# Weaving the two halves of the MLP weights in a fused attention and mixer kernel

## The chip, the cores and the metric

The kernel runs on one core of a Trainium2 chip. The metric is the device time of one execution in microseconds (us). Each TensorE product is two instructions in the trace: a weight load (LDWEIGHTS, row "PEld"), which puts the stationary operand into the array, and a MATMUL (row "PE"), which streams the moving operand past it. The other engines are VectorE (DVE), ScalarE (ACT), GpSimd (POOL) and SyncE (SP), whose queue issues the transfers.

## The reference, cut to what matters

Three layers follow each other. Attention with tanh-capped scores gives x for 2 batches of 448 tokens with 768 channels. The second layer is the one that the change touches:

```python
X = np.fft.fft(np.fft.fft(x, axis=1), axis=2)
u = x + np.real(X)
un = (u - mean(u)) / np.sqrt(var(u) + 1e-06)
x = u + np.maximum(un @ w_ch1, 0.0) @ w_ch2      # w_ch1 768x3072, w_ch2 3072x768
```

The third layer is a gated spatial mixer with weights w_in, w_sg and w_out. The weights w_ch1, w_ch2, w_in and w_out come as 64-bit floats; everything is computed in 32 bits.

## The kernel before, in words

**One product is three.** [...] `product` (L172) issues, for each block of 128 input channels, upper times upper, upper times lower and lower times upper, each with its own weight load. In the MLP the weights are the stationary operand, 128 by 128 words, and the tokens are the moving operand, 448 columns.

**Weights.** `w_ch1` is cut into 24 blocks of 128 columns (`columns`, L844), `w_ch2` into 24 blocks of 128 rows (`rows`, L852). The number f0 of a block runs from 0 to 23 in both; the trace calls both `w_<f0>` (with `raw` and `cvt` behind it for the stages of the conversion). `weight` (L799) makes one block: a transfer of the 64-bit words, then seven steps (`size` to `lower`) which shift and mask the words into 32 bits and write the upper half (`upper`, L828) and the lower half (`lower`, L831) into the tile `w`. That tile holds 768 words of upper halves and behind them 768 words of lower halves in each partition:

```python
w = wpool[tag].tile([P, 2, NP * P], F32R, tag=tag, bufs=W_BUFS[tag], name=tile_name)   # L808
```

`upper` runs on ACT, except for w1_0 to w1_3, w2_0 and w2_1, where it is a DVE copy. `lower` runs on DVE.

**Order.** The MLP is done in six groups of four blocks. In a group, `hidden` (tile h, four blocks of `w_ch1`, L857) and then `mixed` (tile c, four blocks of `w_ch2`, L869) run for batch 0 and batch 1. Each block takes part in 36 products in each of its two roles, so 72 for one f0 and 1728 in all. Group 0 is interleaved by hand with the Fourier transforms and the layer norm of batch 1 (the long list at the end of the `bounded` branch); groups 1 to 5 are ordered by the framework. A weight tile has four buffers per pool (two in "wc"), so a conversion starts when an older block has been read for the last time and its transfer has landed.

**Addresses.** `FILL` (L64) puts small pads between pools. With them, the stationary tile and the moving tile of every product of 448 columns and 128 rows in the MLP start 64 bytes apart, counted modulo 256. In the tile of `v` they start 32 bytes apart. [...]

The functions of the program that the change touches, and what calls them:

Of the kernel before, what the change touches and what calls it, by code (L numbers as in the profile page):

```python
# [13 lines left out]
F32R = mybir.dt.float32r  # L14
# [7 lines left out]
P = 128  # L22
B, H, S, D = 2, 12, 448, 64
C = H * D
NP = H // 2
# [35 lines left out]
W_BUFS = {"wa": 4, "wb": 4, "wc": 2}  # L61


FILL = {"const": 288, "wb": 96, "normed0": 224, "hidden0": 96, "wc": 96}  # L64
EDGE, GATE_ROW, TABLE_ROW = 160, 192, 3776


# [21 lines left out]
def f32(ap):  # L89
    return ap.bitcast(F32)  # L90
# [9 lines left out]
def common_part(ctx, tc, q, k, cap):  # L100
# [5 lines left out]
    edge = ctx.enter_context(tc.tile_pool(name="edge", bufs=1, side="right"))  # L106
    fill = const.tile([P, FILL["const"] // 4], F32, tag="fill", bufs=1, name="fill_const")
    ident = const.tile([P, P], F32, name="ident")
# [23 lines left out]
def attention_mixers_kernel(ctx, tc, bounded, common, q, k, v, cap, w_ch1, w_ch2, w_in, g_ln, w_sg, b_sg, w_out,  # L132
                            t1, t2, out):
    nc = tc.nc
    w_ch1, w_ch2, w_in, w_out = (w.bitcast(U32) for w in (w_ch1, w_ch2, w_in, w_out))
# [4 lines left out]
    def fill(pool, name):  # L140
        t = pool.tile([P, FILL[name] // 4], F32, tag="fill", bufs=1, name=f"fill_{name}")
        nc.gpsimd.memset(t[:, 0:1], 0.0)
# [651 lines left out]
    def fetch(tile_name, src, lead, width):  # L794
        raw = wraw.tile([P, 2 * NP * P], U32, tag="raw", bufs=2, name=f"{tile_name}raw")
        sp.dma_start(raw[:, :2 * lead * width].rearrange("p (k f) -> p k f", k=lead), src)
        return raw

    def weight(tile_name, src, lead, width, tag, lo_engine=None, pin=False, raw=None, hi_copy=None, pieces=None):  # L799


        n = lead * width
        if raw is None:
            raw = fetch(tile_name, src, lead, width)
        words = raw[:, :2 * n].rearrange("p (n w) -> p n w", w=2)
        low, high = words[:, :, 0], words[:, :, 1]
        c = wraw.tile([P, NP * P], U32, tag="cvt", bufs=2, name=f"{tile_name}cvt")[:, :n]
        w = wpool[tag].tile([P, 2, NP * P], F32R, tag=tag, bufs=W_BUFS[tag], name=tile_name)  # L808

        def size():  # L810
            first_op = act.activation(f32(c), f32(high), AF.Abs)
            if pin:
                tc.keep_in_program_order(first_op)

        def clamp():
            vec.tensor_scalar(f32(c), f32(c), LEAST, MOST, op0=ALU.max, op1=ALU.min)

        def shift():
            vec.tensor_scalar(c, c, 5, 2, op0=ALU.logical_shift_left, op1=ALU.logical_shift_right)

        def top():
            vec.scalar_tensor_tensor(c, high, 0xC0000000, c, op0=ALU.bitwise_and, op1=ALU.bitwise_or)

        def bottom():
            vec.scalar_tensor_tensor(c, low, 29, c, op0=ALU.logical_shift_right, op1=ALU.bitwise_or)

        def upper():
            (hi_copy or act.copy)(w[:, 0, :n], f32(c))  # L828

        def lower():  # L830
            (lo_engine or vec).tensor_tensor(w[:, 1, :n], f32(c), f32(w[:, 0, :n]), op=ALU.subtract)  # L831

        steps = size, clamp, shift, top, bottom, upper, lower
        if pieces is None:
            for step in steps:
                step()
        else:
            pieces.extend(steps)
        return w

    def column_block(src, f0):
        return src[:, 2 * f0 * P:2 * (f0 + 1) * P].rearrange("(k p) f -> p k f", p=P)

    def columns(src, f0, name, tag="wa", **how):  # L844

        w = weight(f"{name}{f0}", column_block(src, f0), NP, P, tag, **how)
        return w.rearrange("p a (k f) -> p a k f", k=NP)

    def row_block(src, f0):
        return src[f0 * P:(f0 + 1) * P, :].unsqueeze(1)  # L850

    def rows(src, f0, name, tag="wb", **how):  # L852

        return weight(f"{name}{f0}", row_block(src, f0), 1, C, tag, **how)


    def hidden(b, g, un, w1, hs, chunks=range(GF)):  # L857
# [170 lines left out]
    def opened(*names):  # L1028
        pools = [ctx.enter_context(tc.tile_pool(name=name, bufs=1)) for name in names]
        for pool, name in zip(pools, names):  # L1030
            if name in FILL:
                fill(pool, name)
        return pools if len(pools) > 1 else pools[0]

    wraw = opened("wraw")
    wpool = {"wa": opened("wa")}
# [11 lines left out]
    with ExitStack() as fctx:  # L1048
# [8 lines left out]
        with ExitStack() as actx:  # L1057
# [8 lines left out]
            if bounded:  # L1066
                f, n0 = fourier(0, fp, t2sb, POOL_FOLDS[0]), layer_norm(0, fp)
                f1, n1 = fourier(1, fp, t2sb), layer_norm(1, fp)
                raws, pieces = {}, {}
                do = functools.partial  # L1070

                def get(*key):
                    name, i = key
                    src = column_block(w_ch1, i) if name == "w1_" else row_block(w_ch2, i)
                    raws[key] = fetch(f"{name}{i}", src, *((NP, P) if name == "w1_" else (1, C)))

                def convert(*key):
                    name, i = key
                    how = dict(raw=raws[key], pieces=pieces.setdefault(key, []))
                    if name == "w1_":  # L1080
                        w1.append(columns(w_ch1, i, name, hi_copy=vec.tensor_copy, **how))
                    else:
                        w2.append(rows(w_ch2, i, name, hi_copy=None if i > 1 else vec.tensor_copy, **how))
# [48 lines left out]
            else:  # L1132
# [5 lines left out]
                for n in range(n_pairs + 2):  # L1138

                    if n + 2 < n_pairs:  # L1140
                        raws[n + 2] = load(*pairs[n + 2])
                    for step, group in enumerate(GROUPS):
                        if n < n_pairs:
                            es[n, step] = score(*pairs[n], step, *ready[n])
                        if 0 < n <= n_pairs:
                            if step == 0:
                                pTs[n - 1] = ap.tile([CP, NT, ROWS * P], F32, tag="pT", bufs=2, name=f"pT{n - 1}")
                            for i, r in enumerate(group):
                                flip(*pairs[n - 1], r, i, es[n - 1, step], pTs[n - 1])
                        if step == 1 and n > 1:  # L1150
                            values(*pairs[n - 2], raws[n - 2][2], pTs[n - 2])
                            if pairs[n - 2] == (0, NP - 1):
                                side = norm(0, fp, t2sb)
                        if step == 1 and n + 1 < n_pairs:
                            ready[n + 1] = prepare(*pairs[n + 1], n + 1, raws[n + 1])
                        for f in range(GF):
                            if (n, step) == W1_AT[f]:
                                w1.append(columns(w_ch1, f, "w1_", lo_engine=pool, pin=f < 2))
                        run(side, SIDE_STEPS[step])
# [119 lines left out]
        else:  # L1279
# [10 lines left out]
            run(main, 2)  # L1290
            run(side, 2)
            w2.extend(rows(w_ch2, f, "w2_", pin=True) for f in range(GF))
            w1_next = [columns(w_ch1, GF + f, "w1_", "wc", pin=True) for f in range(2)]
            for n_side, n_main in PLAN:
                run(main, n_main)
# [14 lines left out]
    for g in range(1, NG):  # L1310
# [24 lines left out]
        if g == 2:  # L1335
# [3 lines left out]
            sp.dma_start(sg_raw[:, :, :S], rows_sg)  # L1339
            sp.dma_start(sg_raw[:, :, S:], rows_sg[:, :, NB * P:])  # L1340
        w2 = [rows(w_ch2, g * GF + f, "w2_") for f in range(GF)]
        for b in range(B):
            if g == NG - 1:
# [9 lines left out]
    for j in range(2):  # L1353
        for k in range(2):
            block = w_in[k * HC:(k + 1) * HC, 2 * DH + j * 512:2 * DH + (j + 1) * 512]
            w = weight(f"wv{j}{k}", block.rearrange("(k p) f -> p k f", p=P), 3, 256, "wb")
            wv.append(w.rearrange("p a (k f) -> p a k f", k=3))
# [45 lines left out]
```

## Time and profile before

| | |
|---|---|
| median of 2 runs | 615.39 us (615.38 to 615.41) |
| the profiled execution's own time | 616.05 us |
| its span in the trace | 614.3 us |
| granted TensorE clock, mean | 0.998 |
| PE busy | 603.2 us, 98% |
| PEld busy | 517.6 us, 84% |
| DVE busy | 481.1 us, 78% |
| ACT busy | 271.0 us, 44% |
| POOL busy | 111.5 us, 18% |

A MATMUL's duration in the trace is longer than the time until the next one starts, since they are pipelined. The distance from start to start is therefore read from a run of equal instructions: the time from the first start to the last end, less the duration of one, divided by the count less one. In the chain of waits such a run stands as one piece with its count, which is already that distance times the count.

### The profile page before, as it was taken

To read this page: it belongs to the slowest core of one execution; us is meant where nothing else is said; L and a number is where in the kernel's file an instruction comes from. 1 tells how busy PE (TensorE), PEld (TensorE's weight loads), DVE (VectorE), ACT (ScalarE), POOL (GpSimd) and SP (SyncE) were. 2 spreads that over 40 slices of the span, in tenths; PEclk is the share of its full clock that TensorE was granted. 3 is DMA by queue.
4 is the path that set the end of the run, shared out by engine and by line. 5 is a ranking of instruction groups with operands and counts; after the bars stand their busy time and mean duration, and the time that the engine had idled before them with its cause. 6 is when DMAs were issued, how large, how long until landed. Compare 5 with 4: busy or idle time off the path is not lost.

```text
span 614.3 us, 8700 instructions
## 1 busy us (share of the span) xinstructions
PE 603.2 (98%) x3324; PEld 517.6 (84%) x3324; DVE 481.1 (78%) x764; ACT 271.0 (44%) x374; POOL 111.5 (18%) x156
## 2 busy tenths in 40 slices
PE   7999999999999999999999999999999999999995
PEld 5455566469999999999999999999999999989985
DVE  2698988889876898998938973885579899898461
ACT  5999876932132344334304422350245254543231
POOL 2889895552000000000000000000000010100000
PEclk9999999999999999999999999999999999999999
DMA  6766732201100447444413440453044204100123
GB/s 161 178 172 168 204 91 53 100 0 53 53 1 16 155 155 205 159 157 156 154 52 103 130 179 0 126 177 110 1 161 147 104 24 140 44 1 2 35 71 80
DMA packets 70034, 62.61 MB, mean 102 GB/s; under 512 B 36256, under 2 KB 63840, under 8 KB 69984
## 3 DMA queue, kind: packets, MB, share of 16 engines
q1 hardware_dynamic: 69056, 61.74, 32.7%
q8 instruction: 28, 0.46, 0.3%
q10 hardware_dynamic: 928, 0.23, 0.2%
q14 instruction: 22, 0.18, 0.1%
HBM read 59.21 MB, written 2.75 MB: 101 GB/s over the span
## 4 chain that ended last, share of the span: by engine, by line
PE 89%; DVE 4%; ACT 2%; DMA 2%; issue 1%; POOL 1%; SPq 0%; DVEq 0%; ACTq 0%
PE c L178 28%; PE h L178 26%; PE v L178 5%; PE o L666 5%; PE out L178 5%; PE u L178 5%; PE s L640 4%; PE sg L178 2%; PE st L307 2%; PE st L266 1%; PE tr L605 1%; PE den L679 1%; PE den L677 1%; DMA w_0raw<-in_moe_w_ch 1%; DMA w_2raw<-in_moe_w_ch 1%
## 5 line engine op out<-in xcount | busy, mean ns | idle before, releaser
L178 PE MATMUL c<-h,w 128*128 128x448 f32 x864 | 175.5, 363 | 0.0
L178 PE MATMUL h<-un,w 128*128 128x448 f32 x864 | 174.9, 362 | 0.0
L178 PEld LDWEIGHTS c<-h,w 128*128 128x128 f32 x864 | 161.8, 187 | 11.5 <-DVE h L899 0.4
L178 PEld LDWEIGHTS h<-un,w 128*128 128x128 f32 x864 | 161.7, 187 | 11.5 <-ACT xT L671 0.7
L874 DVE TENSOR_TENSOR xT<-xT,c 128x448 f32<-128x448 f32 x60 | 36.9, 616 | 33.4 <-PE c L178 33.4
L1347 POOL CAST x<-x 128x384 fp32r<-128x384 f32 x2 | 2.8, 1423 | 315.5 <-PE u L178 315.5
L645 ACT ACTIVATE e<-s,tanh_scale 128x896 f32<-128x896 f32 (+1 forms) x48 | 40.9, 927 | 10.6 <-PE s L640 10.5
L666 PE MATMUL o<-e,v 128*64 128x448 f32 x192 | 42.0, 553 | 0.0
L658 POOL TENSOR_TENSOR t<-t,e 128x224 f32<-128x224 f32 x48 | 41.7, 897 | 0.1
L654 POOL TENSOR_TENSOR t<-e 128x224 f32<-128x224 f32 x48 | 40.6, 876 | 3.3 <-POOL mix L629 2.0
L649 ACT ACTIVATE e<-e,cap_pos 128x1792 f32<-128x1792 f32 (+1 forms) x24 | 37.9, 1632 | 0.0
L865 ACT ACTIVATE h<-h 128x448 fp32r<-128x448 f32 x40 | 21.7, 542 | 26.6 <-DVE h L866 16.5
L178 PE MATMUL out<-gated,wo 128*128 128x448 f32 x144 | 30.9, 367 | 0.0
L178 PEld LDWEIGHTS v<-wv,x 128*128 128x128 f32 x252 | 29.7, 188 | 0.1
L178 PE MATMUL v<-wv,x 128*128 128x256 f32 x252 | 29.7, 279 | 0.0
L178 PE MATMUL u<-x,wu 128*128 128x448 f32 x144 | 29.1, 362 | 0.0
L640 PEld LDWEIGHTS s<-qT,kT 64*128 64x128 f32 x216 | 19.4, 188 | 10.9 <-ACT e L649 4.2
L178 PEld LDWEIGHTS u<-x,wu 128*128 128x128 f32 x144 | 26.9, 187 | 1.8
L178 PEld LDWEIGHTS out<-gated,wo 128*128 128x128 f32 x144 | 26.3, 188 | 2.0 <-ACT gated L169 0.2
L640 PE MATMUL s<-qT,kT 64*128 64x448 f32 x216 | 27.3, 385 | 0.6 <-ACT qT L613 0.2
L866 DVE SCALAR_TENSOR_TENSOR h<-h,h 128x448 fp32r<-128x448 f32 x40 | 24.7, 618 | 1.8 <-ACT h L865 1.8
L666 PEld LDWEIGHTS o<-e,v 128*64 128x64 f32 x192 | 11.5, 136 | 16.4 <-issue 14.2
(405 smaller groups left out, 864.3 us busy)
## 6 DMA issues: line engine op xcount, KB each, us to landing
out<-res SPq DMA_DIRECT2D x12, 224.0 KB, 2.5
k<-in_k SPq DMA_DIRECT2D x22, 112.0 KB, 3.6
q<-in_q SPq DMA_DIRECT2D x22, 112.0 KB, 4.0
t<-dft_channels SPq DMA_DIRECT2D x8, 291.0 KB, 5.3
v<-in_v SPq DMA_DIRECT2D x24, 96.0 KB, 2.6
w_0raw<-in_moe_w_ch SPq DMA_DIRECT2D x2, 768.0 KB, 5.1
w_1raw<-in_moe_w_ch SPq DMA_DIRECT2D x2, 768.0 KB, 5.5
w_2raw<-in_moe_w_ch SPq DMA_DIRECT2D x2, 768.0 KB, 5.0
```

The lines of the kernel that those rows point to most:

```text
L178: pe.matmul(ps, lhs(i, a), rhs(i, b), start=start and m == 0, stop=stop and m == last)
L266: pe.matmul(ps[:HS, m * 256:m * 256 + NE], fold[:, i, m * HS:(m + 1) * HS], tab[:, i, :], start=i == 0, stop=i == 2)
L307: pe.matmul(sums[c][:, n * 256 + i:n * 256 + 2 * HS:2], src[:, i, sel], t2sb[:HS, n, i, :], start=True, stop=True)
L640: pe.matmul(ps[:, i, :S], t[lo:hi, x, at:at + P], qT[lo:hi, y, :], start=m == 0, stop=m == 2)
L645: act.activation(es[n][:, 2 * step:2 * step + nr], sums.pop((n, step))[:, :nr, :S], AF.Tanh, scale=tanh_scale)
L649: act.activation(part, part, AF.Exp, scale=cap_pos)
L654: pool.tensor_tensor(t[:, j, q], es[n][:, j, q], es[n][:, 2 + j, q], op=ALU.add)
L658: pool.tensor_tensor(ts[n][:, j, q], ts[n][:, j, q], es[n][:, 4 + j, q], op=ALU.add)
L666: pe.matmul(os[n][halfs[j], :S], vts[n % 3][:, j, i], es[n][:, 2 * i + j if i < 3 else 6], start=i == 0, stop=i == 3)
L865: act.activation(h[:, 0], ps[:, i, :S], AF.Relu)
L866: vec.scalar_tensor_tensor(h[:, 1], ps[:, i, :S], 0.0, f32(h[:, 0]), op0=ALU.max, op1=ALU.subtract)
L874: vec.tensor_tensor(u[:, c, :], u[:, c, :], ps[:, :S], op=ALU.add)
```

## The change

The tile of a weight block is 64 words (256 bytes) longer per partition. A new function, `halves_of`, gives the view of it in which the two halves are written and read. For `w_in` and `w_out` the view is as before. For a block f0 below 16 the view starts 4·f0 words (16·f0 bytes) into the tile and the halves alternate word by word: upper word 0, lower word 0, upper word 1, and so on. A weight load of 128 words thus takes every second word of 1024 bytes, where it took 512 bytes in a row. For the blocks 16 to 23 the halves stay one behind the other, and the view starts 16 times 0, 1, 2, 3, 4, 6, 8 and 12 bytes into the tile. No instruction is added or removed, and no loop changes.

```diff
+PLAIN = (0, 1, 2, 3, 4, 6, 8, 12)
...
+    def halves_of(w, place):
+
+        if place is None:
+            return w[:, :2 * NP * P].rearrange("p (a n) -> p a n", a=2)
+        at, woven = place
+        part = w[:, 4 * at:4 * at + 2 * NP * P]
+        return part.rearrange("p (n a) -> p a n", a=2) if woven else part.rearrange("p (a n) -> p a n", a=2)
+
...
-        w = wpool[tag].tile([P, 2, NP * P], F32R, tag=tag, bufs=W_BUFS[tag], name=tile_name)
+        w = halves_of(wpool[tag].tile([P, 2 * NP * P + 64], F32R, tag=tag, bufs=W_BUFS[tag], name=tile_name), place)
...
+    def place_of(src, f0):
+
+        if src is w_in or src is w_out:
+            return None
+        return (f0, True) if f0 < 16 else (PLAIN[f0 - 16], False)
+
...
-        w = weight(f"{name}{f0}", column_block(src, f0), NP, P, tag, **how)
+        w = weight(f"{name}{f0}", column_block(src, f0), NP, P, tag, place=place_of(src, f0), **how)
...
-        return weight(f"{name}{f0}", row_block(src, f0), 1, C, tag, **how)
+        return weight(f"{name}{f0}", row_block(src, f0), 1, C, tag, place=place_of(src, f0), **how)
```

## Rows read from the trace of the kernel before

**Rows 1.** The page, part 4: the chain's share by engine.
```profile
PE 89%; DVE 4%; ACT 2%; DMA 2%; issue 1%; POOL 1%; SPq 0%; DVEq 0%; ACTq 0%
```

**Rows 2.** Chain of waits, 200 to 500 us: start us, us, piece.
```profile
236.41 28.80 PE c L178 x144
265.21 28.81 PE h L178 x144
...
410.81 28.80 PE c L178 x144
439.61 28.81 PE h L178 x144
```

**Rows 3.** Busy time by stretch: PE, PEld, DVE, ACT, POOL, PEclk, DMA share, GB/s.
```profile
15.00:125.00 110.00, 108.90 (x673) 61.43 (x671) 94.08 (x141) 95.38 (x111) 87.22 (x114) 1.00 0.50 135
207.00:265.00 58.00, 58.00 (x291) 54.35 (x291) 52.03 (x77) 22.28 (x31) 0.00 (x0) 1.00 0.54 173
265.00:323.00 58.00, 58.00 (x292) 54.35 (x291) 44.79 (x65) 18.03 (x26) 0.00 (x0) 1.00 0.38 128
```

**Rows 4.** Groups by line: shapes, count | busy us, mean ns | idle before, releasers.
```profile
L187 PE MATMUL s<-mean_w 128*128 128x256 bf16 x12 | 1.5, 272 | 0.0
L266 PE MATMUL st<-t,fold 128*113 128x194 f32 x96 | 16.8, 329 | 0.2 <-DVE fold L254 0.2
L307 PE MATMUL st<-t2sb,back 113*128 113x113 f32 x48 | 5.9, 277 | 0.0
L178 PE MATMUL v<-wv,x 128*128 128x256 f32 x252 | 29.7, 279 | 0.0
```

**Rows 5.** Timeline of PE: start us, us, instructions of one kind in a row.
```profile
11.46 1.47 PE L187 MATMUL s<-mean_w 128*128 128x256 bf16 x12
...
151.44 2.14 PE L266 MATMUL st<-t,fold 128*113 128x194 f32 x12
...
160.27 2.84 PE L307 MATMUL st<-t2sb,back 113*128 113x113 f32 x24
...
553.13 12.77 PE L178 MATMUL v<-wv,x 128*128 128x256 f32 x108
```

**Rows 6.** Groups of DVE, 190 to 614 us.
```profile
L822 DVE SCALAR_TENSOR_TENSOR w_6cvt<-w_6raw,w_6cvt 128x768 uint32<-128x768 uint32 x2 | 1.9, 956 | 0.0
L831 DVE TENSOR_TENSOR w<-w_10cvt,w 128x768 fp32r<-128x768 f32 x2 | 1.9, 956 | 0.2 <-ACT w L828 0.2
```

**Rows 7.** Lines 828 and 811, instruction by instruction: ns min/median/max, starts.
```profile
L828 DVE CAST w<-w_0cvt x2: 659/664/669, 22.4 to 87.0; 128x768 fp32r<-128x768 f32 x2
L828 DVE CAST w<-w_1cvt x2: 829/864/900, 35.1 to 117.1; 128x768 fp32r<-128x768 f32 x2
L828 ACT CAST w<-w_4cvt x2: 828/830/833, 199.8 to 220.9; 128x768 fp32r<-128x768 f32 x2
...
L811 ACT ACTIVATE w_6cvt<-w_6raw x2: 902/906/910, 206.2 to 224.9; 128x768 f32<-128x768 f32 x2
```

**Rows 8.** Timeline around the fourth block of group 1, both roles.
```profile
217.01 0.95 DVE L831 TENSOR_TENSOR w<-w_7cvt,w 128x768 fp32r<-128x768 f32 x1
...
236.25 2.96 PE L178 MATMUL c<-h,w 128*128 128x448 f32 x14
236.43 0.96 DVE L831 TENSOR_TENSOR w<-w_7cvt,w 128x768 fp32r<-128x768 f32 x1 [0.90 <-ACT w L828]
```

**Rows 9.** Groups of DVE, 88 to 160 us: a write of every second word (L283).
```profile
L314 DVE TENSOR_TENSOR xT<-xT,st 128x225 f32<-128x225 f32 x8 | 3.1, 384 | 1.4 <-PE st L307 1.4
L283 DVE TENSOR_TENSOR pq<-st,late 113x194 f32<-113x194 f32 x8 | 2.4, 350 | 0.0
```

More of the change, by code (lines that the diff above doesn't have):

```diff
@@ L797, in fetch, with weight @@
         return raw
-    def weight(tile_name, src, lead, width, tag, lo_engine=None, pin=False, raw=None, hi_copy=None, pieces=None):
+    def halves_of(w, place):
[4 more added lines that the diff above has]
+        return part.rearrange("p (n a) -> p a n", a=2) if woven else part.rearrange("p (a n) -> p a n", a=2)
+    def weight(tile_name, src, lead, width, tag, lo_engine=None, pin=False, raw=None, hi_copy=None, pieces=None,
+               place=None):
         n = lead * width
```

## The prediction

> **What bounds the kernel now.** I read the chain of waits first: TensorE carries 89% of it [rows 1]. From 200 to 500 us the chain is nothing but runs of 144 products, each run 28.80 or 28.81 us [rows 2], so one product takes 200.0 ns from start to start, without a gap, whatever DVE and ACT do beside it. The busy table by stretch comes second: PE is full in those stretches, and DVE has 52.03 of 58 us in group 1 and less after it [rows 3]. So the change is worth what it does to those 200.0 ns, times the products that it touches, plus what it does to the conversions where they are nearly late.
>
> [...]
>
> [...]
>
> **The change, part by part.**
>
> 1. *Woven loads.* Blocks 0 to 15, 72 products each: 1152 of the 1728. No row shows a weight load that takes every second word, so I bound the price. [...] I take 0. The nearest rows for the load itself are DVE's reads of every second word: L822 takes 956 ns, L831 with whole rows of words takes 956 ns as well [rows 6]. [...]
>
> 2. *Plain blocks moved by 16 to 192 bytes.* Seven of the eight (block 16 stays at 0), 7 × 72 = 504 products. [...] I take 0: in the `st` products with 113 columns the operands start at changing distances, and 24 of them in a row hold 111.3 ns on average [rows 5]; they don't show a full-rate stream, so the bounds stay in the range.
>
> 3. *`upper` on DVE, six copies.* The four of w_0 and w_1 have medians of 664 and 864 ns [rows 7]. They might drop to the pace of a two-input operation, 956 ns [rows 6]: 2 × 292 + 2 × 92 = 0.8 us, and the two of w1_2 and w1_3 add at most 0.6 us. Not below 0, since the same words are moved. They lie in 15 to 125 us, where DVE has 94.08 of 110 us [rows 3] and the chain is mostly PE. Nearest row for the write: L283 writes every second word, 194 of them, in 350 ns; L314 writes 225 in a row in 384 ns [rows 9]. The 31 words fewer save 34 ns, 1.1 ns each, about the 1.2 ns per word of L822 (956 / 768, its fixed part included), so the step costs nothing. What may be lost is the copy's faster pace. I put 0.2 of the 1.4 us on the path.
>
> 4. *`upper` on ACT, 26 of its 42 copies become woven.* The nearest row for a step of two words on ACT is a read: 906 against 830 ns for a copy in a row [rows 7], so 0 to 76 ns each. Cost 0: ACT is idle for more than half of group 1 [rows 3]. The cover is thin at one place: block 7 as `w_ch1` is first read at 207.44 + 54 × 0.2 = 218.2 us and its lower half 0.4 us later, and it is ready at 217.96 [rows 2, 8]; as `w_ch2` it is the tenth product of the stage at 236.25, so 238.05, lower half 238.45, and ready at 237.39 [rows 8]. 0.7 and 1.1 us to spare against 0.08; if that cover went, PE would wait for the difference, once for each.
>
> 5. *`lower` on DVE.* It reads one woven half and writes the other; both steps are priced at 0 by rows 6 and 9. The transfers and SP's queue are not touched.
>
> Sum: 616.05 (the profiled execution's own time, 614.3 of span and 1.75 around it) + 0 + 0 + 0.2 = 616.25. The profiled execution is 0.66 us over the median of the runs, so in runs that is **615.6 us**.
>
> **The rivals.**
>
> *Full pace without loss (faster), 0.20.* [...] A part of this gain (only some of the 16 distances are good), 605 to 612 us, I give 0.12.
>
> *Twice the lines, twice the loss (slower), 0.17.* [...]
>
> *The load becomes the bound (slower), 0.06.* [...]
>
> *The plain blocks alone feel their new places, 0.05:* up to 5.5 us to either side, 610 to 621.
>
> *No price, my forecast, 0.40:* 615.6, by itself 612 to 619.
>
> **How the numbers follow.** 2% of the median, about what a measurement of this kernel can tell from no change, is 12.3 us: 603.1 and 627.7 us are the borders. The first rival ends astride the lower border; I count half of it, 0.10, as faster. The second ends just above the upper one; I count 0.10 of its 0.17 as slower, with all of the third: 0.16. Within 2%: 0.74. The range takes in the forecast, the partial gain, most of the first rival and the second, and leaves out the load as the bound: 602.5 to 628.5.
>
> **What would show it.** In the chain of waits after, the runs of 144 products of groups 1 to 3 (woven) against groups 4 and 5 (plain): my forecast has 28.8 us in all of them. [...] L828 on DVE should lie between today's time and 956 ns, on ACT between 830 and 906. I would be wrong if the start-to-start time in the woven groups moves by more than 3 ns, or if PE waits near 218 or 238 us.

## The result and the profile after

The changed kernel takes **622.89 us** (622.45 to 623.34, 2 runs) against 615.39: a ratio of **1.0122** with an interval of 1.0078 to 1.0165. That is slower, by less than the 2% of the prediction's border, and inside its range; the interval leaves no doubt that it moved. The profiled execution took 622.45 us, with 620.6 us of span at a mean granted clock of 0.998; the span is 6.3 us longer than before's. In the kernel after, the product stands in L179, `upper` in L838 and `lower` in L841.

The chain of waits of the kernel after, 200 to 510 us (start us, us, piece), answers to [rows 2]:

```profile
208.26 29.39 PE h L179 x144
237.65 29.36 PE c L179 x144
267.01 29.18 PE h L179 x144
296.20 29.27 PE c L179 x144
325.47 14.68 PE h L179 x72
340.15 1.54 PE sgT L1344 x16
341.68 14.67 PE h L179 x72
356.36 29.57 PE c L179 x144
385.92 29.31 PE h L179 x144
415.24 29.27 PE c L179 x144
444.51 29.32 PE h L179 x144
473.83 29.14 PE c L179 x144
```

Each piece still follows the one before it without a gap, but none has 28.80 us: a product comes every 202.4 ns (29.14 / 144) to 205.3 ns (29.57 / 144). The pieces of groups 1 to 3, which are woven, add up to 176.12 us, those of groups 4 and 5, plain, to 117.04 us. The same pieces added up to 172.86 and 115.22 us before, so the loss is 3.3 and 1.8 us. Group 0 loses 0.57 us: from the first `h` product to the first run above it is 76.25 us, and was 75.68. That is 5.7 of the 6.3 us. The stage ahead of the MLP is 0.1 us later, and the rest comes behind the last piece of the chain (`res` ends 5.99 us before the span does, 5.39 before).

Where the chain carries PE only, the engines beside it tell whether PE is starved. Timeline of PE in the kernel after, 208 to 240 us (start us, us, instructions in a row, idle time in brackets if any), answers to [rows 8]:

```profile
208.10 29.55 PE L179 MATMUL h<-un,w 128*128 128x448 f32 x144
237.49 2.82 PE L179 MATMUL c<-h,w 128*128 128x448 f32 x13
```

No bracket stands behind either row: PE waits neither near 218 nor near 238 us, the two places where the prediction had called the cover thin. Busy time by stretch of the kernel after, columns as in [rows 3]:

```profile
207.00:265.00 58.00, 58.00 (x286) 55.22 (x285) 52.00 (x75) 22.85 (x30) 0.00 (x0) 1.00 0.53 166
```

The granted clock is 1.00 as before [rows 3], and PE is still full, with 286 MATMULs in the 58 us where 291 stood. A full busy column says nothing about the pace.

Groups by line of the kernel after (columns as in [rows 4]), first MATMULs, then weight loads:

```profile
L179 PE MATMUL c<-h,w 128*128 128x448 f32 x864 | 178.2, 366 | 0.0
...
L179 PEld LDWEIGHTS c<-h,w 128*128 128x128 f32 x864 | 166.2, 193 | 9.9 <-PE c L179 0.2 <-issue 0.2
L179 PEld LDWEIGHTS h<-un,w 128*128 128x128 f32 x864 | 165.8, 192 | 10.4 <-ACT xT L672 0.7
...
L179 PEld LDWEIGHTS u<-x,wu 128*128 128x128 f32 x144 | 26.9, 187 | 1.8
```

The recorded load is 192 to 193 ns on the mean of woven and plain blocks, where the load of `u`, untouched, has 187. The plain blocks have no part in that: in groups 4 and 5 (390 to 500 us), where all are plain, the loads of `h` and `c` have 188, in the woven groups (210 to 380 us) 195.

Lines 838 and 841 of the kernel after, instruction by instruction (ns min/median/max, starts), answer to [rows 7] and [rows 6]; w_16 belongs to a plain block:

```profile
L838 DVE CAST w<-w_0cvt x2: 671/672/672, 22.4 to 87.1; 128x768 fp32r<-128x768 f32 x2
L838 DVE CAST w<-w_1cvt x2: 836/870/903, 35.2 to 117.1; 128x768 fp32r<-128x768 f32 x2
L838 ACT CAST w<-w_4cvt x2: 887/889/891, 200.3 to 221.9; 128x768 fp32r<-128x768 f32 x2
...
L838 ACT CAST w<-w_15cvt x2: 889/924/960, 298.2 to 332.5; 128x768 fp32r<-128x768 f32 x2
L838 ACT CAST w<-w_16cvt x2: 835/838/842, 345.4 to 384.1; 128x768 fp32r<-128x768 f32 x2
...
L841 DVE TENSOR_TENSOR w<-w_4cvt,w x2: 951/952/952, 201.6 to 223.1; 128x768 fp32r<-128x768 f32 x2
```

Over the 24 copies of the blocks 4 to 15, ACT has a mean of 901 ns, where it was 830: 70 ns more, and nine of the 26 woven copies on ACT lie above the 906 ns of the forecast. No product waits for one, so the conversions cost the kernel what was forecast, and nearly all of the loss is in the pace of the products.

### The profile page after: what moved, and what is told of

It is laid out like the page before. It is cut to its first block, busy times and chain, and to the rows that moved or that the text cites. A ratio compares the mean times of both kernels' runs of the same rounds, so it can differ in the third digit from the quotient of the medians.

```text
span 620.6 us, 8700 instructions
## 1 busy us (share of the span) xinstructions
PE 608.3 (98%) x3324; PEld 525.7 (85%) x3324; DVE 483.2 (78%) x764; ACT 272.6 (44%) x374; POOL 111.5 (18%) x156
## 4 chain that ended last, share of the span: by engine, by line
PE 90%; DVE 4%; DMA 2%; ACT 1%; issue 1%; POOL 1%; SPq 0%; DVEq 0%; ACTq 0%
PE c L179 28%; PE h L179 26%; PE o L667 5%; PE v L179 5%; PE out L179 5%; PE u L179 5%; PE s L641 5%; PE sg L179 2%; PE st L308 2%; PE st L267 1%; PE den L678 1%; PE den L680 1%; PE tr L606 1%; DMA w_0raw<-in_moe_w_ch 1%; DMA w_2raw<-in_moe_w_ch 1%
## 5 line engine op out<-in xcount | busy, mean ns | idle before, releaser
L179 PE MATMUL c<-h,w 128*128 128x448 f32 x864 | 178.2, 366 | 0.0
L179 PE MATMUL h<-un,w 128*128 128x448 f32 x864 | 177.9, 366 | 0.0
L179 PEld LDWEIGHTS h<-un,w 128*128 128x128 f32 x864 | 165.8, 192 | 10.4 <-ACT xT L672 0.7
L179 PEld LDWEIGHTS c<-h,w 128*128 128x128 f32 x864 | 166.2, 193 | 9.9 <-PE c L179 0.2
L179 PE MATMUL out<-gated,wo 128*128 128x448 f32 x144 | 30.9, 367 | 0.0
L179 PE MATMUL v<-wv,x 128*128 128x256 f32 x252 | 29.7, 279 | 0.0
L179 PEld LDWEIGHTS v<-wv,x 128*128 128x128 f32 x252 | 29.7, 188 | 0.1
L179 PE MATMUL u<-x,wu 128*128 128x448 f32 x144 | 29.1, 362 | 0.0
L179 PEld LDWEIGHTS u<-x,wu 128*128 128x128 f32 x144 | 26.9, 187 | 1.8
L179 PEld LDWEIGHTS out<-gated,wo 128*128 128x128 f32 x144 | 26.4, 188 | 2.0 <-ACT gated L170 0.2
```

The lines of the kernel that those rows point to most:

```text
L179: pe.matmul(ps, lhs(i, a), rhs(i, b), start=start and m == 0, stop=stop and m == last)
```

## The experiments

In what follows the *distance* of a product is where its moving tile starts less where its stationary tile starts, in bytes modulo 256. Before, it is 64 everywhere in the MLP; the change moves the stationary tile by 16 bytes per block and so lowers the distance by as much. It is counted from the start of the view; in a woven block the lower halves (what is left of a word when its upper half, its value cast to `fp32r`, is subtracted), which every third product loads, start 4 bytes further. Each kernel is the changed one with the edit shown. The time from start to start is a chain piece divided by its count. e1 to e4 were run 4 or 10 times; e5 to e9 have one run each and are read by their pieces.

**e1_tile_only: the longer tile, nothing moved, nothing woven.**

```diff
-        return (f0, True) if f0 < 16 else (PLAIN[f0 - 16], False)
+        return 0, False
```

> All blocks plain at place 0: of the change only the 256 bytes added to each weight tile stay. If the distance between the weight load and the stream (modulo 256) sets the price, every run of 144 products is back at 28.80 us and the time at 615.4 us. If the longer tile or the moved pools cost something by themselves, it stays above 617 us.

Measured: 615.57 us, ratio 1.0007 (0.9996 to 1.0018). Chain of waits of e1, one run of `h`; those of `c` have 28.80 us:

```profile
206.96 28.81 PE h L179 x144
```

The 256 bytes more per tile, and the pools behind them that move, cost nothing. What is left is the weave and the place of the view in its tile.

**e2_moved_plain: every block at the place of the change, none woven.**

```diff
-        return (f0, True) if f0 < 16 else (PLAIN[f0 - 16], False)
+        return (f0, False) if f0 < 16 else (PLAIN[f0 - 16], False)
```

> No weave; the blocks 0 to 15 keep their places of 0 to 240 bytes, plain. Theory place: the weave adds nothing on the mean of all places, so 1656 moved products cost about 3.5 ns each, +5.8 us, 621 us, as the changed kernel. Theory weave (the woven loads are what costs in blocks 0 to 15): only the eight plain blocks cost, +1.7 us, 617 us.

Measured: 620.91 us, ratio 1.0088 (1.0067 to 1.0109). Chain of waits of e2:

```profile
207.41 29.41 PE h L179 x144
236.81 29.35 PE c L179 x144
...
384.89 29.30 PE h L179 x144
```

These are nearly the pieces of the kernel after (29.39, 29.36, 29.31) without any weave; those of groups 1 to 3 add up to 175.95 us against 176.12. Moving the view by a few times 16 bytes costs as much by itself as moving and weaving together.

**e3_woven_at_0: 16 blocks woven, none moved.**

```diff
-        return (f0, True) if f0 < 16 else (PLAIN[f0 - 16], False)
+        return 0, f0 < 16
```

> Blocks 0 to 15 woven, every block at place 0. Theory place in its simple form (the distance alone counts, woven or not): 200.0 ns everywhere, 615.4 us. Theory weave: 1152 products at +3.5 ns, 619.5 us. Place with a best distance of its own for woven loads: in the changed kernel the woven block at place 0 came at 204.1 ns, so 1152 x 4.1 = +4.7 us, 620 us, and groups 4 and 5 at 28.80 us.

Measured: 618.95 us, ratio 1.0054 (1.0035 to 1.0074). Chain of waits of e3, a woven group and a plain one:

```profile
208.27 29.29 PE h L179 x144
237.56 29.29 PE c L179 x144
...
385.54 28.82 PE h L179 x144
414.36 28.80 PE c L179 x144
```

At distance 64 the weave costs 3.4 ns a product (29.29 / 144 = 203.4), and 1152 × 3.4 = 3.9 us, against 3.8 us measured (618.95 less 615.17 of the kernel before on the same chip). So the weave costs something here; whether it does so everywhere is the next question.

**e4_woven_at_8: all 24 blocks woven, all moved by 128 bytes, distance 192.** In the kernel after, the woven block 8, at this distance, had come at 200.5 ns in `h`, by the starts of its 36 products, where the `h` pieces of groups 1 to 3 have a mean of 203.5 ((29.39 + 29.18 + 14.68 + 14.67) / 432).

```diff
-        return (f0, True) if f0 < 16 else (PLAIN[f0 - 16], False)
+        return 8, True
```

> All 24 blocks woven, all at 128 bytes (place 8, distance 192 modulo 256, the best woven place in the changed kernel: 200.4 ns as w_ch1). Place with a best distance of its own for woven loads: 1728 x 0.4 = +0.7 us, 616 us, runs of 144 at 28.85 us. Place in its simple form (a plain block at distance 192 came at 202.3): +4 us, 619.4 us. Theory weave: 1728 x 3.5 = +6 us, 621.4 us. Below 615 us would mean that weaving everything leaves room under 200 ns.

Measured: 616.11 us, ratio 1.0014 (1.0004 to 1.0024). Chain of waits of e4:

```profile
131.37 15.09 PE h L179 x72
...
353.50 28.80 PE c L179 x144
382.30 28.81 PE h L179 x144
```

and its weight loads by line:

```profile
L179 PEld LDWEIGHTS h<-un,w 128*128 128x128 f32 x864 | 166.7, 193 | 7.4 <-ACT xT L672 0.7 <-DVE h L882 0.5
```

With everything woven, the 200.0 ns are back. The load is recorded at 193 ns, 6 more than a plain one's 187, and the products don't feel it. No run of products has a pace better than 200.0 ns. Timeline of PE in e4, the second run of `h` in group 2:

```profile
279.63 2.67 PE L179 MATMUL h<-un,w 128*128 128x448 f32 x12 [0.17 <-DVE h L882]
```

At full pace, PE waits once for the conversions' engine, 0.17 us: DVE writes the last lower half of w_11 just before, at 278.08 to 279.04 us, and comes to the `h` that is due after it. The product there starts 528 ns after the one before and the next one 312 ns later, instead of 200 each: 0.44 us in all. One run differs: the very first 72 products of `h` came at 206 to 207 ns in 70 of 71 gaps; e9 takes that up.

**e5_plain_steps: all plain, each group of `w_ch2` at one place of its own, `w_ch1` moved by 8 bytes per block.** This keeps the four blocks that alternate in `c` at one distance.

```diff
-        part = w[:, 4 * at:4 * at + 2 * NP * P]
+        part = w[:, at:at + 2 * NP * P]
...
-        return (f0, True) if f0 < 16 else (PLAIN[f0 - 16], False)
+        if src is w_ch1:
+            return 2 * f0, False
+        return (0, 8, 16, 32, 48, 56)[f0 // GF], False
```

> No weave. Block f0 of w_ch1 starts 8 x f0 bytes into its tile; of w_ch2 all four blocks of a group share a place: 0, 32, 64, 128, 192, 224 bytes in groups 0 to 5 (distances 64, 32, 0, 192, 128, 96 modulo 256). Theory distance: the runs of c in groups 1 to 5 differ from each other, none is under 28.80 us, and the blocks of w_ch1 at places met before repeat their prices (distance 160 about 200.5 ns, 192 about 202.3, 32 about 205.5). Theory neighbours (the change of place from one block to the next is what costs): all uniform runs of c are back at 28.80 us. If some distance between the 16-byte steps is better than 64, a block comes under 199.5 ns.

Measured: 620.59 us (before on the same chip 615.63). Chain of waits of e5, `c` of groups 1 to 5, at the distances 32, 0, 192, 128 and 96:

```profile
236.11 29.75 PE c L179 x144
...
295.31 29.18 PE c L179 x144
...
355.33 29.11 PE c L179 x144
...
413.73 29.38 PE c L179 x144
...
472.41 29.57 PE c L179 x144
```

206.6, 202.6, 202.2, 204.0 and 205.3 ns: the loss isn't made by neighbours at different places, since it stays when all four are at the same one. The same stream comes at five paces as the weights' place changes. Each pace is steady: at 32 all gaps but the first are 206 or 207 ns, and at 128 the gaps 209, 196, 203, 212 and 200 ns repeat to the piece's end.

**e6_woven_steps: the same, woven; `c` at the distances 64, 0, 208, 192, 176 and 128.**

```diff
-        part = w[:, 4 * at:4 * at + 2 * NP * P]
+        part = w[:, at:at + 2 * NP * P]
...
-        return (f0, True) if f0 < 16 else (PLAIN[f0 - 16], False)
+        if src is w_ch1:
+            return 2 * f0, True
+        return (0, 16, 28, 32, 36, 48)[f0 // GF], True
```

> All blocks woven. w_ch1 in steps of 8 bytes as in the kernel before this one; w_ch2 one place per group: distances 64, 0, 208, 192, 176, 128 in groups 0 to 5. Theory distance, with woven loads having a table of their own: c at 192 (group 3) is 28.80 us, the others lie between 28.80 and 29.8 us (64 gave 29.28). Theory neighbours: all c of groups 1 to 5 at one value. [...]

Measured: 620.97 us (before 615.63). Chain of waits of e6, `c` of groups 1 to 5:

```profile
236.90 29.29 PE c L179 x144
...
295.56 29.28 PE c L179 x144
...
355.71 28.80 PE c L179 x144
...
413.70 29.28 PE c L179 x144
...
472.33 29.53 PE c L179 x144
```

The best of these distances for a woven load is 192; 208 and 176, 16 bytes to either side, cost 3.3 ns each. It isn't the only good one: in the same kernel's `h`, block 15, at distance 200, settles at gaps of 200 ns in both batches. At 192 a plain load costs 2.2 ns (e5), a woven one nothing; at 64 it is the other way about (200.0 ns plain in e1, 203.4 woven in e3).

**e7_all_by_32: plain, nothing moved within its tile, but the pad ahead of the pools 32 bytes longer.** It shifts weight tiles and moving tiles together, except for the `h` tiles of batch 1, which end up 32 bytes from their weights.

```diff
-FILL = {"const": 288, "wb": 96, "normed0": 224, "hidden0": 96, "wc": 96}
+FILL = {"const": 320, "wb": 96, "normed0": 224, "hidden0": 96, "wc": 96}
...
-        return (f0, True) if f0 < 16 else (PLAIN[f0 - 16], False)
+        return 0, False
```

> No weave, every block at place 0, but the first pad is 32 bytes longer, so the pools on the left side move by 32 bytes together: un, h of batch 0 and all weights. h of batch 1 lies on the right side and stays: its distance to w_ch2 becomes 32, and so does that of part of the gate's products. Theory distance: h in both batches and c of batch 0 stay at 200.0 ns; only the half of a c run that belongs to batch 1 rises, to 203 to 206 ns, so c runs of 144 take 29.0 to 29.3 us and the time is 617 to 618.5 us. Theory absolute address: the h runs move too.

Measured: 618.44 us (before 615.63). Chain of waits of e7:

```profile
207.46 28.81 PE h L179 x144
236.27 29.27 PE c L179 x144
```

`h` keeps its 200.0 ns at new addresses. In `c` the loss of 0.47 us lies in one half of the piece, batch 1: (29.27 − 14.40) / 72 = 206.5 ns, the pace of e5 at the same distance. So for this shift it is the distance that counts, not where the tiles lie.

**e8_narrow: the load made short, nothing woven, nothing moved.** In groups 1 to 5, the products of a sum between its first and its last load only 32 columns of weights in `h` and 64 in `c`, which leaves most of the result out. The stream stays at 448 columns.

```diff
-                pe.matmul(ps, lhs(i, a), rhs(i, b), start=start and m == 0, stop=stop and m == last)
+                k = narrow if narrow and 0 < m < last else P
+                pe.matmul(ps[:k], lhs(i, a)[:, :k], rhs(i, b), start=start and m == 0, stop=stop and m == last)
...
-        return (f0, True) if f0 < 16 else (PLAIN[f0 - 16], False)
+        return 0, False
```

> No weave, place 0; 16 of 18 products of a block of w_ch1 load only 32 columns of weights, and 10 of 12 products of a c tile only 64 (in groups 1 to 5 and wherever the same functions serve), so most of the result is left out; the streams are the same. [...] Theory stream alone: 200.0 ns and 28.80 us in all of them.

Measured: 619.89 us (before 615.63). Chain of waits of e8, and its weight loads by line (the calls of `h` pass `narrow=32`, those of `c` `narrow=64`):

```profile
207.18 29.54 PE h L180 x144
236.72 29.04 PE c L180 x144
```

```profile
L180 PEld LDWEIGHTS c<-h,w 128*64 128x64 f32 x600 | 80.5, 134 | 37.5
L180 PEld LDWEIGHTS h<-un,w 128*32 128x32 f32 x640 | 69.1, 108 | 59.1
```

In `h` the load shrinks from 188 to 108 ns in the records, and a product takes 205.1 ns instead of 200.0 (201.7 in `c`): slower, where I had looked for 200.0 ns or less. What there might have been to win is an estimate: the bf16 stream of 256 columns comes every (1.47 − 0.27) / 11 = 109 ns [rows 4, 5], at that pace 448 columns would take 190.8 ns, and 9.2 of the 200.0 ns are over. At distance 64, then, a shorter load wins back none of the 9.2 ns. No other distance was tried with the short load, and its products also write fewer rows of the result, so what the 9.2 ns are stays open.

**e9_start: e4 with another beginning.** Three bf16 products whose result isn't used are issued ahead of the first `h` product. The edit is shown against e4.

```diff
-                h0.prod(0, range(3))
+                h0.prod(0, range(3), idles=3)
```

> All blocks woven at place 8, as in the kernel whose later runs came at 200.0 ns but whose first run of 72 products of h (group 0, batch 0) came at 206.7 ns throughout (15.09 us), with the same distance of 192. Here three bf16 products that nothing uses stand ahead of that first run. Theory start (stream and load fall into step, and into which step depends on how the run began): the run of 72 leaves 15.09 us, for 14.4 or 14.65 us. Theory place alone (something in the places of group 0 differs that the distance modulo 256 does not hold): it stays at 15.09 us.

Measured: 615.87 us (before 615.47). Timeline of PE in e4, then in e9, at the start of the MLP:

```profile
131.30 15.16 PE L179 MATMUL h<-un,w 128*128 128x448 f32 x72
```

```profile
131.20 0.50 PE L188 MATMUL h<-mean_w 128*128 128x256 bf16 x3
131.46 14.68 PE L179 MATMUL h<-un,w 128*128 128x448 f32 x72
```

The same 72 products at the same places now come at 200 ns in 66 of 71 gaps, 0.48 us less in all. Whether the kernel gains by it, one run of e9 on another chip can't tell: it is 0.40 us over the kernel before there, e4's median 0.94 us over it. But the beginning decided the pace of this run, 206 to 207 or 200 ns, at one and the same distance.

e2 shows the same within one kernel. Timeline of PE in e2, block 20 of `w_ch1`, plain at distance 0, in batch 0 and then in batch 1:

```profile
443.30 3.87 PE L179 MATMUL h<-un,w 128*128 128x448 f32 x18
457.99 3.81 PE L179 MATMUL h<-un,w 128*128 128x448 f32 x18
```

By their starts these are 206.5 and 202.5 ns a product, each held through the 18, with the same weights at the same place. What differs is the batch's moving tile, which makes no difference in e1, and what ran before. In block 4, at distance 0 as well, it is the other way about: 202.8 ns in batch 0 and 206.6 in batch 1. So one distance had two paces here.

No kernel beat the one before: e1 and e4 equal it within 0.15%, and in no run of products of any of them was the pace better than 200.0 ns.

## Why the prediction's range held and its price was wrong, step by step

*Parts 1 and 2, the price of a woven load and of a moved plain one, taken as 0: these failed.* "I would be wrong if the start-to-start time in the woven groups moves by more than 3 ns": it moved by 176.12 / 864 − 200.0 = 3.8 ns in groups 1 to 3, and by 3.2 ns in groups 4 and 5. The value taken, 0, was wrong in both. The range held the time since its ends, and the 5.5 us to either side of the rival with the plain blocks, go back to an estimate of mine of 11 ns in a product that might vanish or double. No run shows that term; what the runs showed in its place are products 0 to 6.7 ns late, and no run of products ahead of 200.0 ns. That the time also stayed within 2% was luck, since no term of the sum knew of this loss. And 2% is more than a measurement here needs: the interval of the ratio is 0.4% to either side, so a loss of 1.2% is clear of it. Group 0 adds its 0.57 us, and the three together are 5.7 of the 6.3 us.

The reason I gave for part 2 was the `st` products [rows 5], which keep 111.3 ns on average at changing distances. I said there that they don't show a full-rate stream (with 194 columns they take 164.5 / 194 = 0.85 ns a column, where `v` takes 116.7 / 256 = 0.46, from (2.14 − 0.33) / 11 = 164.5 and (12.77 − 0.28) / 107 = 116.7 ns in [rows 4, 5]), and then took their value all the same. Each of their gaps is 111 or 112 ns, but at 0.85 ns a column 113 columns would take 95.8 ns (an estimate), and some 15 ns more pass, so that row can't show a stream that is held up by a few ns. The MLP's products come up to 6.7 ns late. For part 1 I leaned on DVE's reads of every second word [rows 6]. They say how long one engine takes, and that carried over well (the woven load is recorded at 193 ns in e4, 6 more than the 187 before). What they can't say is what a load and a stream beside each other cost.

What stood behind both was that each edit was priced by itself. e2 and e3 show the two edits apart: moving alone costs 5.74 us over the 22 blocks that it moves (block 0 and block 16 stay at 0; the expectation had counted 23), 5.74 / (22 × 72) = 3.6 ns a product, weaving alone 3.4 ns, and e4 shows both at once, at one place for all, for next to nothing. So the prices don't add. In the `c` pieces the price went with the distance from stationary to moving start (202.2 to 206.6 ns in e5, 200.0 to 205.1 in e6, 200.0 and 206.5 for the halves of a piece in e7), in `h` with the beginning of a run too (202.5 and 206.5 ns in e2, 206 to 207 and 200 in e4 and e9). No run tests by itself that the distance counts modulo 256 bytes; the products of one piece, whose starts differ by multiples of 256, come at one pace (at distance 32 in e5, 206 or 207 ns in all gaps but the first). The kernel before has 64 everywhere by its pads, and no plain load at another distance was better; I took that for a property of the layout and didn't ask what it was worth.

*Part 3, `upper` on DVE: right.* 664 became 672 and 864 became 870 ns; the copy kept its pace, and the six cost less than the 0.2 us that were put down. *Part 4, ACT: right in its cost here, with the bound and a place missed.* 830 became 901 ns on the mean, +70 of the bound of 76, but nine of 26 copies went over 906 ns, the longest to 960. The thin cover held near 218 and 238 us all the same. In the kernel after that is no full proof, since its products are late themselves; in e4, where they come every 200.0 ns, it held at these two places too, and gave way at a third that the prediction hadn't named, 279.63 us, for 0.17 us of idle time and 0.44 us in the starts. *Part 5: right*, 952 ns.

**The rivals.** *Full pace* fell for the distances tried: none, woven or not, brought a run of products under 200.0 ns in ten kernels. *Twice the lines, twice the loss* fell as a law, since the woven load at distance 192 costs nothing, though it takes its words from 1024 bytes as at 64, where it costs 3.4 ns. *The load as the bound* fell with e4: its woven load is recorded at 193 ns against 187, and the products come every 200.0 ns all the same. *The plain blocks alone* was half right: they feel their places (in e5 nothing but the weights' addresses was changed from the plain kernel e1, and the same stream takes from 202.2 to 206.6 ns in `c` instead of 200.0), and the woven ones do as well (200.0 to 205.1 ns in e6).

What stays open: what the 9.2 ns over the pace of the bf16 stream are, at the best distance too; by what mechanism the distance works; and why the beginning of a run matters. The recorded MATMULs are longer where products come late (366 ns on the mean against 362 and 363 before), and the plain loads of groups 4 and 5 hardly are (188 against 187), so it is the stream that is stretched there and not the load, but that is a reading of the records and no more.

## What to carry to other kernels

A change of a tile's layout is a change of addresses, and moving the view alone cost 5.74 us here (e2). Where weight loads run beside a stream, as in the MLP (PE busy for 58.00 us of 58, PEld for 54.35, in [rows 3]), note the distance between their starts before, keep it, or measure its price with a kernel that only shifts a pad, in more than one run of products, since one distance had two paces here (202.5 and 206.5 ns at distance 0). Test one uniform place at a time, as a mixture of places gives a mean in which nothing can be read. And an engine that is full in the busy table, without a gap in the chain, can still lose 2% in its period (58.00 us of 58 after the change, with 204.1 and 203.9 ns a product instead of 200.0): divide the run by its count.

## What the runs showed of the hardware

Products of 448 columns with 4-byte words, loads and streams from start to start, `c` pieces with one distance each, divided by 144 (for 64 plain, the piece of e1; for 64 woven, that of e3):

| distance, bytes modulo 256 | 0 | 32 | 64 | 96 | 128 | 176 | 192 | 208 |
|---|---|---|---|---|---|---|---|---|
| plain, ns (e1, e5) | 202.6 | 206.6 | 200.0 | 205.3 | 204.0 | | 202.2 | |
| woven, ns (e3, e6) | 203.4 | | 203.4 | | 205.1 | 203.3 | 200.0 | 203.3 |

The `h` blocks, 18 products at a time, show that this table is not the whole of it. Plain blocks reach gaps of 200 ns at distance 160 as well (block 20 in e5, block 10 in e2), at 16 block 6 of e5 has them where block 19 of e2 comes at 203.4 ns, and at 0 one block has 202.5 and 206.5 ns (e2). A woven block reaches them at 200 (block 15 in e6). DVE copies words into every second place at the pace of a copy in a row (672 against 664 ns for 768 words), while ACT pays 70 ns for it on the mean of 24 copies (901 against 830). And a shorter weight load (32 columns, recorded at 108 ns) made the stream no faster at distance 64: 205.1 ns.
